# A hand-planned attention order with its copy queue, a start of its own for ten units, and MLP products placed between the last transposes

## The chip, the cores and the metric

The kernel runs on one core of a Trainium2 chip. The metric is the device time of one execution in microseconds (us). TensorE does the matmuls and transposes, VectorE and ScalarE read its results out of PSUM, GpSimd works on SBUF alone, and SyncE issues most of the transfers. Each engine works through its own list of instructions in the order in which the program was written; between engines there are only semaphores.

## The reference

```python
q_assign = argmax(q_n @ c_n)            # 16 clusters, per head
k_assign = argmax(k_n @ c_n)
mask = q_assign[:, :, :, None] == k_assign[:, :, None, :]
scores = where(mask, 0.125 * q @ k.T, -1e9)
attn_out = softmax(scores) @ v          # 2 batches, 8 heads, 768 x 64, fp32
x = attn_out as (1536, 512)
h = max(max(x @ w1, x @ w2), x @ w3);   x = h @ w_out           # 512 -> 768 -> 512
h = x @ w_in;  out = max(0.01 * h, h) @ w_out2                  # 512 -> 2048 -> 512
```

All of it is fp32, and the weights are read as 64-bit words and taken apart into two fp32r halves on the chip.

## The kernel before

The work has two parts. The attention part has 16 head slices, taken as 8 pairs of heads (0 to 7). A pair is 6 units, so there are 48 units (n = 0 to 47); a unit is 256 queries of one head against 768 keys. The MLP part then runs the two MLPs over three blocks of 512 tokens, each product as three fp32r matmuls (`three`, L226), with the weight units taken apart beside it (`Weights`, L104).

One unit passes through these steps, which the order tables name with letters. `S0`, `S1` (`scores`, L589, matmuls L601): two score blocks of 128 queries, each of four matmuls, two on the operands q1, k1 and two on q2, k2, which also carry the cluster rows that mask. `M` (`maxima`, L605): the row maximum on VectorE. `X` (`exps`, L610): exp on ScalarE with the sums. `R` (`inverse`, L619): two small VectorE instructions. `Q` (`normal`, L625): scaling on GpSimd. `T0`, `T2`, `T4` (`transposes`, L629): four TensorE transposes each. `E0`, `E2`, `E4` (`out_of_psum`, L640): their copies, by ScalarE, VectorE, ScalarE. `V` (`values`, L651, matmuls L657): 24 matmuls, once for two units. `Y` (`store`, L662): the copy to `acc`. The score blocks have two PSUM buffers (pool `ps_s`), so block i+2 waits for the exp of block i.

A pair is prepared before its first unit. `LD` and `LV` (`load_pair`, L337) load q, k and v from SyncE's queue; q and k have two buffers, v has three. `G`, `C`, `H`, `Na`, `Nb`, `W`, `FA`, `FB`, `O`, `P` (L472 to L518) find each token's cluster and end in the tile `oo`; they use one buffer `e` and one `oh`. `QH`, `KH`, `QL`, `KL` round q and k and form the rests. `D0` and `D1` (`operands`, L526, copies L530) copy the rounded tiles and `oo` into the operand tiles: 10 transfers each (a row with x2 in an order is two), from SyncE's queue. `w` takes one step at the weight unit 0 (`take_apart`, L681; each step is one or two instructions of `piece`, L136), and `F` (`fetch_pieces`, L675) issues the loads `raw` and `low` for it.

The order is written out in tables. `BEGIN` is the list up to the steady state, with dummy matmuls (`I2`, `I4`: `idle`, L769). `ORDER` has one string for each of the six places r of a unit in its pair: for each n the loop at L894 goes through string n % 6; `S0/-3` there means step S0 of unit n+3, and `KH+2` means KH of the pair two ahead. `ONCE` puts further steps ahead of a named one, `END` stands last. Nothing is reordered later (the schedule is manual), so the place of an item in these strings is its place on its engine's list. What an item waits for is the data and the buffers.

The lines of `ORDER` that matter here are r = 0 and r = 1, which hold `D0+1 ... LD+3 LV+2` and `D1+1`: SyncE's queue has the loads of q, k and v between the two halves of a pair's copies.

Of the kernel before, what the change touches and what calls it, by code (L numbers as in the profile page):

```python
# [17 lines left out]
P = 128  # L18
B, H, S, D = 2, 8, 768, 64
C = 16  # L20
NP = H // 2
NPAIR = B * NP
NQ = S // P
G = 256
# [10 lines left out]
SCALE = 0.125  # L35
BIG = 2.0**100
ORDER = (
    "R/-1 E2/1 X1/-2 Nb+2 D0+1 Q1/0 Q0/-1 R/-2 T4/1 S0/-3 T0/0 E4/1 S1/-3 E0/0 M0/-3 LD+3 LV+2 X0/-3 "
    "M1/-3 T2/0 T4/0 X1/-3 Q1/-1",
    "T0/0 S0/-3 Q0/-1 Y/4 E2/1 QH+2 T2/0 S1/-3 W+2 FA+2 M0/-3 D1+1 F+0 Q1/-1 M1/-3 R/-2 X0/-3 Q0/-2 V/2 "  # L40
    "E2/0 E4/1 X1/-3",
    "S0/-3 E0/1 w+0 Q1/-1 w+0 T4/1 KH+2 M0/-3 S1/-3 E4/1 M1/-3 R/-2 T0/0 QL+2 X0/-3 Y/3",
    "X1/-2 T2/1 T4/1 S0/-3 V/2 E0/1 Q0/-1 E4/1 S1/-3 FB+2 M0/-3 X0/-3 T0/0 E0/0 Q1/-1 E2/1 T2/0 M1/-3 "
    "S0/-4 T4/0 E2/0 T0/-1 R/-2",
    "X1/-2 S1/-3 T2/0 E4/1 G+3 E0/0 Q0/-1 Q1/-1 T4/0 M0/-3 X0/-3 R/-2 M1/-3 S0/-4 E2/0 X1/-3 C+3",
    "T0/0 S1/-3 E4/1 KL+2 O+2 H+3 Y/4 w+0 M0/-3 Q0/-1 M1/-3 Na+3 T2/0 E0/0 P+2 X0/-3 w+0 w+0 V/2",
)

BEGIN = (
    "Zaq LDq Zal Zak LDk Zaj Zam Gq I2 Gk Zar I2 Naq Nbq Wq FAq FBq Zbq UQ Zbk CQ LV0 I6 Nak "  # L50
# [3 lines left out]
)  # L54

END = "h h h V:47 h h Y:47 h"

ONCE = {
    "M1:3": "KL@1", "X1:3": "D0@1 F", "S1:5": "D1@1", "E0:4": "V:2 Y:2",
    "T0:46": "in x0 x1", "T0:47": "x2 x3 ph h", "T4:47": "h", "E4:47": "oh h",  # L60
}
WAYS = ("ADA", "ADA")
ENGINE = {"QH": "A", "QH@1": "P", "KH": "P", "KL": "P", "KL@0": "D", "W": "P", "W@1": "D"}
# [10 lines left out]
def clustered_attention_mlps(  # L74
# [124 lines left out]
    mlp, m = ctx.enter_context(ExitStack()), {}  # L199

    def open_inputs():

        m["w1"] = mlp.enter_context(tc.tile_pool(name="w1", bufs=1))
        xp = mlp.enter_context(tc.tile_pool(name="xp", bufs=1))
        m["xh"] = [xp.tile([P, KD, TB], F32R, name=f"xh{t}") for t in range(NTB)]
        m["xl"] = [xp.tile([P, KD, TB], F32R, name=f"xl{t}") for t in range(NTB)]

    def open_products():
        m["ps_h"] = mlp.enter_context(tc.tile_pool(name="ps_h", bufs=4, space=PSUM))

    def open_hidden():

        m["tp"] = mlp.enter_context(tc.tile_pool(name="tp", bufs=2))
        m["hp0"] = mlp.enter_context(tc.tile_pool(name="hp0", bufs=1))

    chunks = [[0], [1]] + [[u, u + 1] for u in range(2, U1 + U2, 2)]

# [86 lines left out]
    with ExitStack() as att:  # L304
# [32 lines left out]
        def load_pair(p, what="qkv", queue=nc.sync):  # L337
            s = st.setdefault(p, {})
            for x in what:
                if x == "v":  # L340
                    s["rv"] = vp.tile([P, NQ, 2, D], F32, tag="rv", name=f"rv{p}")
                    src = v[p].rearrange("p (t h d) -> p t h d", t=NQ, h=2)
                else:
                    s["r" + x] = raws.tile([P, S], F32, tag="r" + x, name=f"r{x}{p}")
                    src = (qT if x == "q" else kT)[p]
                queue.dma_start(out=s["r" + x], in_=src)
# [45 lines left out]
        def sims(p, j, spare):  # L392
            s = st[p]
            r = s[("rq", "rk")[j]]
            for t in range(NQ):
                nc.tensor.matmul(
                    spare[:, t * 2 * C : (t + 1) * 2 * C], r[:, t * P : (t + 1) * P],
                    cb[:, p % NP, :], start=True, stop=True,
                )
            if j == 0:  # L400
                s["m"] = sm.tile([P, NQ, 2, 2, 1], F32, tag="m1", name=f"m1_{p}")
                s["e"] = sm.tile([P, NQ, 2, 2, C], F32, tag="e", name=f"e{p}", bufs=1)
# [267 lines left out]
        def scrap(key):  # L670
            if key not in scraps:
                scraps[key] = ps_t.tile([P, 512], F32, tag="t", name=f"scrap{len(scraps)}")
            return scraps[key]
# [7 lines left out]
        def take_apart():  # L681

            if len(taken) < len(fetched):
                c = fetched[len(taken)]
                if c not in pieces:
                    pieces[c] = weights.piece(weights.raw.pop((0, c)), 0, wa, c)
                if next(pieces[c], None) is None:
                    taken.append(c)
# [67 lines left out]
        if True:  # L756
# [12 lines left out]
            def idle(n):  # L769
                for _ in range(n):  # L770
                    nc.tensor.matmul(warm, nought[:, 0:P], nought, start=True, stop=True)
# [42 lines left out]
            def start(op):  # L814

                if op[0] == "I":
                    idle(int(op[1:]))
                elif op[0] == "Z":
                    first_operands("ab".index(op[1]), op[2])
                elif op == "D2":  # L820
                    operands(0, 2, (1,))
                elif op in ("LDq", "LDk"):
                    load_pair(1, op[2], nc.scalar)
                elif op == "LV0":
                    load_pair(0, "v", nc.scalar)
                elif op in ("Gq", "Gk"):
                    sims(0, "qk".index(op[1]), scrap(op))
                elif op in ("Naq", "Nak"):
                    near_max(0, "qk".index(op[2]), scrap("G" + op[2]))
                elif op in ("Nbq", "Nbk"):  # L830
                    near_eq(0, "qk".index(op[2]))
                elif op in ("Wq", "Wk"):
                    weigh(0, nc.vector, "qk".index(op[1]))
                elif op in ("FAq", "FAk"):
                    first_max(0, "qk".index(op[2]))
                elif op in ("FBq", "FBk"):
                    first_eq(0, "qk".index(op[2]))
                elif op in ("UQ", "UK"):
                    onehot_up(0, "QK".index(op[1]), scrap(op))
                elif op == "CQ":  # L840
                    ps = scrap("UQ").bitcast(BF16)[D : D + C, 0:S]
                    nc.scalar.copy(st[0][0][1][D : D + C], ps)
                elif op == "CK":
                    ps = scrap("UK").bitcast(BF16)[D : D + C, 0:S]
                    up = slice(D, D + C)
                    nc.scalar.activation(
                        st[0][0][3][up], ps, AF.Identity, scale=gain[up], bias=base[up]
                    )
                elif op == "OT":
                    for h in range(2):  # L850
                        onehot_T(0, h, scrap(op)[:, 256 * h : 256 * h + 256])
                elif op in ("PA", "PB"):
                    h = "AB".index(op[1])
                    penalties(0, h, scrap("OT")[:, 256 * h : 256 * h + 256])
                elif op == "in":
                    until_scores.close()
                    open_inputs()
                elif op == "oh":
                    until_transposes.close()
                    open_hidden()  # L860
                elif op == "F":
                    fetch_pieces()
                elif op == "ph":
                    until_exps.close()
                    open_products()
                    st["first"] = hidden(0, 0)
                elif op == "h":
                    next(st["first"])
                elif op[0] == "x":
                    split_x(0, (int(op[1]),))  # L870
                else:
                    raise ValueError(op)

            NU = NPAIR * 2 * NG
            begun = BEGIN.split() + END.split()
            begun += ["V:1", "Y:1"]
# [17 lines left out]
            for n in range(-2 * NG, NU + 2 * NG):  # L894
                c, r = divmod(n, 2 * NG)
                for item in ORDER[r].split():
                    if "/" in item:
                        op, by = item.split("/")
                        if 0 <= n - int(by) < NU:
                            ordered(op, n - int(by))  # L900
                    else:
                        op, by = item.split("+")
                        if op in "wF" or 1 <= c + int(by) < NPAIR:
                            ordered(op, c + int(by))
            assert len(taken) == UW // WP

            for op in END.split():
                other(op)
# [70 lines left out]
```

## Time and profile before

| what | us |
|---|---|
| median of 3 executions (lowest, highest) | 731.91 (727.87, 734.37) |
| the profiled execution, its time | 730.9 |
| its span, from the first to the last instruction | 729.0 |
| TensorE busy in the span | 700.5 (96%) |
| mean granted TensorE clock, as a share of full speed | 0.980 |

The span is what the trace shows; 1.9 us of the profiled execution lie around it. A matmul's duration in the trace overlaps with that of the next one, so the chain of waits, which counts only what each one adds, is the better measure of what a group costs. A share of busy time under one, or a granted clock of 0.50 (1.2 GHz in place of 2.4 GHz), shows where TensorE loses time.

### The profile page before, as it was taken

To read this page: it belongs to the slowest core of one execution; us is meant where nothing else is said; L and a number is where in the kernel's file an instruction comes from. 1 tells how busy PE (TensorE), PEld (TensorE's weight loads), DVE (VectorE), ACT (ScalarE), POOL (GpSimd) and SP (SyncE) were. 2 spreads that over 40 slices of the span, in tenths; PEclk is the share of its full clock that TensorE was granted. 3 is DMA by queue.
4 is the path that set the end of the run, shared out by engine and by line. 5 is a ranking of instruction groups with operands and counts; after the bars stand their busy time and mean duration, and the time that the engine had idled before them with its cause. 6 is when DMAs were issued, how large, how long until landed. Compare 5 with 4: busy or idle time off the path is not lost.

```text
span 729.0 us, 10287 instructions
## 1 busy us (share of the span) xinstructions
PE 700.5 (96%) x3730; PEld 559.3 (77%) x3730; DVE 494.2 (68%) x898; ACT 337.5 (46%) x637; POOL 215.8 (30%) x195
## 2 busy tenths in 40 slices
PE   8678998899999989999999999999999999999997
PEld 5466776676777768888888888888888888888886
DVE  6576896777766529878887289878619954983222
ACT  6356776767867645523322124536434432432220
POOL 0445464555553311101110111223222322222220
PEclk9769999999999999999999999999999999999999
DMA  3873468355261005645555045416514541610112
GB/s 110 273 169 102 140 158 202 101 137 136 66 152 66 1 6 197 209 167 169 159 164 173 30 144 170 147 47 215 166 36 144 174 144 35 197 58 1 43 40 90
DMA packets 30081, 89.95 MB, mean 123 GB/s; under 512 B 4784, under 2 KB 5680, under 8 KB 30032
## 3 DMA queue, kind: packets, MB, share of 16 engines
q1 hardware_dynamic: 29600, 88.14, 40.6%
q10 hardware_dynamic: 432, 1.18, 0.5%
q8 instruction: 29, 0.48, 0.3%
q14 instruction: 20, 0.16, 0.1%
HBM read 68.16 MB, written 3.15 MB: 98 GB/s over the span
## 4 chain that ended last, share of the span: by engine, by line
PE 90%; DVE 3%; ACT 2%; DMA 2%; SPq 1%; POOL 1%; issue 1%; ACTq 0%; POOLq 0%; DVEq 0%
PE h L231 13%; PE h L233 13%; PE h L232 13%; PE o L657 10%; PE y L233 8%; PE s L601 8%; PE y L231 8%; PE y L232 8%; PE t L634 7%; DMA k<-oo 2%; SPq L530 1%; ACT ee L613 1%; DVE mx L607 1%; POOL ee L627 1%; PE g L476 1%
## 5 line engine op out<-in xcount | busy, mean ns | idle before, releaser
L265 POOL TENSOR_TENSOR hl<-a,hh 128x512 fp32r<-128x512 f32 x66 | 92.0, 1394 | 353.3 <-ACT hh L264 345.2
L231 PE MATMUL h<-xh,wh 128*128 128x512 f32 x408 | 159.1, 390 | 0.0
L233 PE MATMUL h<-xh,wl 128*128 128x512 f32 x408 | 158.8, 389 | 0.0
L232 PE MATMUL h<-xl,wh 128*128 128x512 f32 x408 | 158.7, 389 | 0.0
L627 POOL TENSOR_SCALAR ee<-ee,rs 128x768 f32<-128x768 f32 x96 | 96.0, 1012 | 135.6 <-DVE rs L622 47.3
L607 DVE TENSOR_REDUCE mx<-s 128x1 f32<-128x768 f32 x96 | 91.3, 954 | 52.4 <-PE s L601 50.9
L601 PE MATMUL s<-k,q 128*128 128x512 f32 (+3 forms) x392 | 99.4, 376 | 14.0 <-DMA k<-oo 8.8
L231 PE MATMUL y<-hh,wh 128*128 128x512 f32 x264 | 102.7, 389 | 0.0
L232 PE MATMUL y<-hl,wh 128*128 128x512 f32 x264 | 102.7, 389 | 0.0
L233 PE MATMUL y<-hh,wl 128*128 128x512 f32 x264 | 102.7, 389 | 0.0
L264 ACT CAST hh<-a 128x512 fp32r<-128x512 f32 x66 | 41.1, 623 | 127.5 <-DVE a L258 76.7
L613 ACT ACTIVATE ee<-s,mx 128x768 f32<-128x768 f32 x96 | 86.6, 903 | 24.3 <-DVE mx L607 23.4
L634 PE MATMUL t<-idf,ee 128*128 128x128 f32 x576 | 81.8, 279 | 8.1 <-POOL ee L627 7.0
L231 PEld LDWEIGHTS h<-xh,wh 128*128 128x128 f32 x408 | 76.6, 188 | 16.5 <-issue 0.8
L233 PEld LDWEIGHTS h<-xh,wl 128*128 128x128 f32 x408 | 76.6, 188 | 16.0
L232 PEld LDWEIGHTS h<-xl,wh 128*128 128x128 f32 x408 | 76.6, 188 | 15.7
L601 PEld LDWEIGHTS s<-k,q 128*128 128x128 f32 (+1 forms) x392 | 63.3, 201 | 29.2 <-ACT ee L613 10.7
L256 ACT COPY a<-h 128x512 f32<-128x512 f32 x66 | 38.6, 586 | 95.7 <-PE h L233 94.1
L634 PEld LDWEIGHTS t<-idf,ee 128*128 128x128 f32 x576 | 67.5, 143 | 19.4 <-POOL ee L627 8.7
L291 DVE TENSOR_TENSOR acc<-y,acc 128x512 f32<-128x512 f32 x72 | 48.6, 685 | 40.5 <-PE y L233 40.5
L260 DVE SCALAR_TENSOR_TENSOR a<-a,h 128x512 f32<-128x512 f32 x48 | 32.9, 684 | 61.8 <-ACT a L256 61.6
L647 ACT COPY et<-t 128x512 f32<-128x512 f32 x96 | 55.0, 592 | 42.1 <-PE t L634 42.0
(100 smaller groups left out, 847.3 us busy)
## 6 DMA issues: line engine op xcount, KB each, us to landing
raw<-in_w SPq DMA_DIRECT2D x56, 512.0 KB, 3.9
low<-in_w SPq DMA_DIRECT2D x56, 511.5 KB, 3.5
q<-qh SPq DMA_DIRECT2D x28, 192.0 KB, 4.2
k<-kh SPq DMA_DIRECT2D x28, 192.0 KB, 4.3
out_T<-acc SPq DMA_DIRECT2D x12, 256.0 KB, 2.0
rq<-in_qT SPq DMA_DIRECT2D x7, 384.0 KB, 5.0
rk<-in_kT SPq DMA_DIRECT2D x7, 384.0 KB, 3.6
rv<-in_v SPq DMA_DIRECT2D x7, 384.0 KB, 4.0
```

Source lines behind the costliest of these rows:

```text
L231: nc.tensor.matmul(ps, ah, bh, start=(k == 0), stop=False)
L232: nc.tensor.matmul(ps, ah, bl, start=False, stop=False)
L233: nc.tensor.matmul(ps, al, bh, start=False, stop=(k == n - 1))
L265: nc.gpsimd.tensor_tensor(hlo[:, f, :], a, hh[:, f, :].bitcast(F32), op=ALU.subtract)
L291: nc.vector.tensor_tensor(a, ps, a, op=ALU.add)
L601: nc.tensor.matmul(ps[:, lo:hi], a[:, c0 : c0 + P], b[:, lo:hi], start=start, stop=not start)
L607: nc.vector.tensor_reduce(mx, un[n]["s", i], axis=AX.X, op=ALU.max, negate=True)
L613: nc.scalar.activation(e, u.pop(("s", i)), AF.Exp, bias=u.pop(("m", i)), scale=1.0, accum_out=u["sum"][:, i, 0:1],)
L627: nc.gpsimd.tensor_scalar(e, e, un[n]["rs"][:, i : i + 1], 1.0, op0=ALU.mult, op1=ALU.mult)
L634: nc.tensor.transpose(ps[:, kk, i * P : (i + 1) * P], u["e"][i][:, (k + kk) * P : (k + kk + 1) * P], idf,)
L647: nc.scalar.copy(out, ps)
L657: nc.tensor.matmul(un[n]["o"][j * D : (j + 1) * D], v[:, t, j, :], done[p, g, j][:, t, :], start=(t == 0), stop=(t == NQ - 1),)
```

## The change

The tables are new. Of `ORDER`, two lines of the diff show the kind of change:

```diff
-    "R/-1 E2/1 X1/-2 Nb+2 D0+1 Q1/0 Q0/-1 R/-2 T4/1 S0/-3 T0/0 E4/1 S1/-3 E0/0 M0/-3 LD+3 LV+2 X0/-3 "
+    "S0/-3 w+0 X1/-2 T0/0 M0/-3 Q0/-1 S1/-3 M1/-3 Q1/-1 T2/0 E4/1 Y/3 D0+1 E0/0 E2/0 X0/-3 G+2 S0/-4",
```

`LD+3` now stands in r = 2, and in place of `LV+2` there is `LV+1` in r = 5; `D0+1` ends r = 0 and `D1+1` begins r = 1. `BEGIN` is written out up to the scores of unit 13, with its own place for each item of the units 0 to 9. The rest of the diff, cut to its core:

```diff
+AFTER = 10
-END = "h h h V:47 h h Y:47 h"
+END = "h h V:47 h h Y:47"
 ONCE = {
-    "M1:3": "KL@1", "X1:3": "D0@1 F", "S1:5": "D1@1", "E0:4": "V:2 Y:2",
-    "T0:46": "in x0 x1", "T0:47": "x2 x3 ph h", "T4:47": "h", "E4:47": "oh h",
+    "T0:45": "in x0 x1 x2 x3", "T0:46": "ph h h", "T4:46": "h h", "T0:47": "h", "T4:47": "h h",
+    "E4:47": "oh",
 }
...
     def open_inputs():
-        m["w1"] = mlp.enter_context(tc.tile_pool(name="w1", bufs=1))
...
+        m["tp"] = mlp.enter_context(tc.tile_pool(name="tp", bufs=2))
+        m["hp0"] = mlp.enter_context(tc.tile_pool(name="hp0", bufs=1))
...
     def open_hidden():
-        m["tp"] = mlp.enter_context(tc.tile_pool(name="tp", bufs=2))
-        m["hp0"] = mlp.enter_context(tc.tile_pool(name="hp0", bufs=1))
+        m["w1"] = mlp.enter_context(tc.tile_pool(name="w1", bufs=1))
...
                         if op in "wF" or 1 <= c + int(by) < NPAIR:
-                            ordered(op, c + int(by))
+                        if op in "wF":
+                            if n >= AFTER:
+                                do(op, 0)
```

In `ONCE`, `in` opens the MLP's input tiles, `x0` to `x3` split the first token block into its fp32r halves, `ph` opens the MLP's PSUM tiles, and each `h` is one step of three matmuls of the first product. The weights' home `w1` opens later and the hidden tiles' home earlier than before. No matmul of attention or of the MLPs is added or taken away; the dummy matmuls fall from 29 to 23.

What stands on three engines before and now:

VectorE (DVE) at the start, from the last rest of pair 0's operands on. `mx` is a row maximum (M), numbered by unit and block; `near1`, `e1`, `oh1` belong to the cluster search of pair 1, `ql1` to its rounding. Before:

```order
L364 TENSOR_TENSOR k2_0_1_227<-rk0_118,k1_0_1_226 64x768
L607 TENSOR_REDUCE mx0_0_273<-s0_263 128x1
L607 TENSOR_REDUCE mx0_1_279<-s1_266 128x1
L607 TENSOR_REDUCE mx1_0_301<-s2_296 128x1
L621 TENSOR_REDUCE rs0_307<-sums0_107 128x2
L622 RECIPROCAL rs0_307<-rs0_307 128x2
L607 TENSOR_REDUCE mx1_1_322<-s3_315 128x1
L497 TENSOR_REDUCE m1_1_312<-near1_324 128x24
```

Now:

```order
L374 TENSOR_TENSOR k2_0_1_227<-rk0_118,k1_0_1_226 64x768
L507 TENSOR_REDUCE m1_1_280<-near1_287 128x24
L513 TENSOR_TENSOR e1_281<-near1_287,m1_1_280 128x384
L371 SCALAR_TENSOR_TENSOR ql1_305<-rq1_189,qh1_283 128x768
L437 TENSOR_TENSOR e1_281<-e1_281,desc_104 128x384
L443 TENSOR_REDUCE m2_1_None_325<-e1_281 128x24
L457 TENSOR_TENSOR oh1_327<-e1_281,m2_1_None_325 128x384
L617 TENSOR_REDUCE mx0_0_354<-s0_263 128x1
L617 TENSOR_REDUCE mx0_1_367<-s1_266 128x1
```

Six instructions of pair 1's cluster search and rounding moved ahead of the first row maximum.

SyncE (SP) in the steady state, around the second half of pair 3's copies (`kl3`, `oo3`) and the load of v (`rv`). Before:

```order
L530 DMA q1_3_1_1153<-ql3_948 64x768
L346 DMA rq5_1192<-in_qT 128x768
L346 DMA rk5_1194<-in_kT 128x768
L346 DMA rv4_1196<-in_v 128x768
L530 DMA k2_3_0_1147<-kl3_1091 64x768
L530 DMA q2_3_0_1145<-oo3_1115 16x384 x2
```

Now:

```order
L356 DMA rv2_1044<-in_v 128x768
L137 DMA raw0_2_1101<-in_w 128x2048
L137 DMA low0_2_1103<-in_w 128x2046
L540 DMA q1_3_0_1146<-qh3_932 64x768
L540 DMA q2_3_0_1147<-qh3_932 64x768
L540 DMA k1_3_0_1148<-kh3_846 64x768 x2
L540 DMA q1_3_0_1146<-ql3_988 64x768
L540 DMA q1_3_1_1155<-qh3_932 64x768
L540 DMA q2_3_1_1156<-qh3_932 64x768
L540 DMA k1_3_1_1157<-kh3_846 64x768 x2
L540 DMA q1_3_1_1155<-ql3_988 64x768
L540 DMA k2_3_0_1149<-kl3_1051 64x768
```

The two halves of a pair's copies now follow one another, and the load of v stands ahead of both and is that of an earlier pair (2 in place of 4).

VectorE at the end of attention. `et` are copies of transposes (E2), `xl0` the split of the first token block, `rs46` and `rs47` the inverses of the last two units. Before:

```order
L649 COPY et44_3068<-t44_2_3045 128x512
L649 COPY et45_3077<-t45_2_3081 128x512
L222 TENSOR_TENSOR xl0_3104<-acc0_64,xh0_3101 128x512 x2
L621 TENSOR_REDUCE rs47_3116<-sums3_110 128x2
L622 RECIPROCAL rs47_3116<-rs47_3116 128x2
L649 COPY et46_3125<-t46_2_3119 128x512
L222 TENSOR_TENSOR xl0_3104<-acc0_64,xh0_3101 128x512 x2
```

Now:

```order
L659 COPY et44_3035<-t44_2_3030 128x512
L232 TENSOR_TENSOR xl0_3057<-acc0_64,xh0_3054 128x512 x4
L631 TENSOR_REDUCE rs46_3079<-sums2_109 128x2
L632 RECIPROCAL rs46_3079<-rs46_3079 128x2
L631 TENSOR_REDUCE rs47_3086<-sums3_110 128x2
L632 RECIPROCAL rs47_3086<-rs47_3086 128x2
L659 COPY et45_3084<-t45_2_3102 128x512
```

The four splits and the last inverse no longer stand behind the copy of unit 45's transposes.

## Rows read from the trace of the kernel before

**Rows 1.** Stages: stretch, length, busy us (PE, PEld, DVE, ACT, POOL), granted clock, DMA share, GB/s
```profile
16.00:62.00 46.00, 35.23 (x175) 25.17 (x175) 29.23 (x52) 21.31 (x44) 21.73 (x20) 0.78 0.76 209
62.00:91.00 29.00, 26.62 (x202) 20.74 (x206) 21.97 (x40) 21.93 (x45) 12.40 (x13) 1.00 0.33 97
91.00:121.00 30.00, 27.98 (x205) 21.26 (x198) 22.49 (x41) 20.23 (x44) 15.28 (x16) 0.94 0.68 170
121.00:152.00 31.00, 28.42 (x208) 21.46 (x207) 22.56 (x41) 21.27 (x45) 16.11 (x16) 0.94 0.65 150
152.00:181.00 29.00, 27.68 (x218) 20.96 (x215) 23.77 (x41) 21.54 (x45) 16.83 (x17) 1.00 0.46 116
206.60:256.00 49.40, 49.29 (x380) 39.00 (x379) 30.81 (x58) 36.32 (x77) 23.21 (x25) 1.00 0.25 64
256.00:272.00 16.00, 13.80 (x96) 9.41 (x95) 5.15 (x9) 6.16 (x14) 2.74 (x2) 1.00 0.00 1
272.00:729.00 457.00, 453.05 (x1998) 374.79 (x1998) 308.69 (x540) 160.56 (x280) 92.03 (x66) 1.00 0.38 125
```

**Rows 2.** TensorE's waits, whole span: us in total, times, longest
```profile
PE s L601 <- DMA k<-oo: 8.8, 5, 2.6
```

**Rows 3.** SyncE's own waits, 58 to 206 us, same columns
```profile
SPq L346 <- PE o L657: 63.6, 5, 17.1
```

**Rows 4.** Chain that ended last, around 112 us: start, us it adds, what
```profile
109.40 2.33 DMA k<-oo
...
112.39 4.43 PE o L657 x24
```

**Rows 5.** The same chain where nothing waits, at the full clock
```profile
242.30 0.71 PE s L601 x4
243.01 1.31 PE t L634 x12
...
246.17 2.74 PE o L657 x24
```

**Rows 6.** The same chain at the start, two pieces at the lower clock, the first V
```profile
33.42 1.65 PE s L601 x4
...
44.03 0.85 PE t L634 x4
...
59.22 2.79 PE o L657 x24
```

**Rows 7.** TensorE in order of time at the start, with its idle time before
```profile
16.38 1.85 PE L601 MATMUL s<-k,q 128*128 128x512 f32 x8 [0.54 <-ACT ee L613]
...
20.76 2.61 PE L634 MATMUL t<-idf,ee 128*128 128x128 f32 x11 [0.55 <-POOL ee L627]
...
29.87 0.33 PE L634 MATMUL t<-idf,ee 128*128 128x128 f32 x1 [3.46 <-POOL ee L627]
```

**Rows 8.** Single microseconds of the start, columns as in rows 1
```profile
23.00:24.00 1.00, 1.00 (x5) 0.90 (x4) 0.00 (x0) 0.59 (x1) 0.00 (x0) 0.53 0.95 359
...
47.00:48.00 1.00, 1.00 (x6) 0.90 (x6) 0.97 (x5) 0.81 (x2) 0.41 (x1) 0.58 0.45 108
```

**Rows 9.** VectorE in order of time at the start
```profile
19.50 0.55 DVE L497 TENSOR_REDUCE m<-near 128x24 f32<-128x384 f32 x1
...
20.75 1.17 DVE L427 TENSOR_TENSOR e<-e,desc 128x384 f32<-128x384 f32 x1
...
28.09 0.96 DVE L361 SCALAR_TENSOR_TENSOR ql<-rq,qh 128x768 fp32r<-128x768 f32 x1
```

**Rows 10.** ScalarE, in order of time: its last reading of pair 0's k
```profile
14.47 0.84 ACT L353 ACTIVATE k<-rk 64x768 fp32r<-64x768 f32 x1
```

**Rows 11.** Loads of k (`rk`) from issue to landing, first 100 us
```profile
DMA to landing us min/median/max: 3.3/3.7/6.2
```

**Rows 12.** The chain that ended last, at the end of attention
```profile
255.03 0.60 PE t L634 x4
...
261.39 0.98 PE t L634 x7
```

More of the change, by code (lines that the diff above doesn't have):

```diff
@@ L37 @@
 ORDER = (
-    "R/-1 E2/1 X1/-2 Nb+2 D0+1 Q1/0 Q0/-1 R/-2 T4/1 S0/-3 T0/0 E4/1 S1/-3 E0/0 M0/-3 LD+3 LV+2 X0/-3 "
[L39 to L46, printed above, removed]
[9 rows of a table added]
 )
 BEGIN = (
-    "Zaq LDq Zal Zak LDk Zaj Zam Gq I2 Gk Zar I2 Naq Nbq Wq FAq FBq Zbq UQ Zbk CQ LV0 I6 Nak "
[3 rows of a table removed]
-)
-END = "h h h V:47 h h Y:47 h"
+    "Zaq LDq Zal Zak LDk Zaj Zam Gq I2 Gk Zar I2 Naq Nbq Wq FAq FBq Zbq UQ Zbk CQ LV0 I6 Nak Nbk Wk FAk FBk  "
[12 rows of a table added]
+)
+AFTER = 10
+END = "h h V:47 h h Y:47"
 ONCE = {
-    "M1:3": "KL@1", "X1:3": "D0@1 F", "S1:5": "D1@1", "E0:4": "V:2 Y:2",
-    "T0:46": "in x0 x1", "T0:47": "x2 x3 ph h", "T4:47": "h", "E4:47": "oh h",
+    "T0:45": "in x0 x1 x2 x3", "T0:46": "ph h h", "T4:46": "h h", "T0:47": "h", "T4:47": "h h",
+    "E4:47": "oh",
 }
@@ L823, in start @@
                     load_pair(1, op[2], nc.scalar)
+                elif op == "w":
+                    take_apart()
                 elif op == "LV0":
@@ L902, in clustered_attention_mlps @@
                         op, by = item.split("+")
-                        if op in "wF" or 1 <= c + int(by) < NPAIR:
+                        if op in "wF":
+                            if n >= AFTER:
+                                do(op, 0)
+                        elif 1 <= c + int(by) < NPAIR:
                             ordered(op, c + int(by))
```

23 rows, old and new, of tables (BEGIN, ORDER) are left out of this document.

## The prediction

> **What bounds the kernel now.** I read the stages first, because 96% busy over the span hides where the rest is lost [rows 1]. From 272 us on TensorE is busy 453.05 of 457.00 us at full clock, with the same 1998 matmuls' worth of MLP work before and after the change, so nothing can be won there. The two pairs of attention from 206.6 to 256, for which nothing is prepared any more, are as dense: 49.29 of 49.40 us. What is lost lies in three places. From 16 to 62 us TensorE is busy 35.23 of 46.00 us, and at a mean clock of 0.78. From 62 to 181 us it is idle for 2.38, 2.02, 2.58 and 1.32 us in four stretches, 8.30 in all, and two of them have a clock of 0.94. From 256 to 272 us, where attention ends, it is idle for 2.2 us.
>
> Then the waits tell what stands behind the middle loss. TensorE waits five times for the copies of `oo` into the operands, 8.8 us in all [rows 2]. SyncE, which issues them, stood for 63.6 us in five waits on TensorE's V [rows 3]: that is `LV+2`, which wants a buffer of v that the pair before last still reads, and behind it in the queue stand the copies of `D1+1`. In the chain the wait ends in 2.33 us of transfer, and the V behind it takes 4.43 us [rows 4], where one at full clock takes 2.74 [rows 5]: the idle time let the clock fall to the lower level, which cost another 1.69 us. That happens in two of the stretches, the ones with 0.94.
>
> At the start it is a chain through all engines (score, maximum, exp, next score), with the clock on top. After 3.46 us without work [rows 7] the clock fell, and it was back only just before 48 us [rows 8]. At the lower level a score block adds 1.65 us to the chain and a group of four transposes 0.85 [rows 6], against 0.71 and 1.31/3 = 0.44 [rows 5].
>
> **The middle.** The change takes `LV+2` away from between the copies. `LV+1` in r = 5 asks for a buffer whose last V lies a whole pair back, so it should not wait, and `LD+3` now stands behind `D1+1`. SyncE is not tied to the other engines' places: once D0 is free of `rv` it can issue both halves as soon as their data is there, well ahead of the first score of the pair. The waits for `oo` then go with the lower clock they cause: at most 8.30 us of idle time and 2 x 1.69 = 3.4 us of clock, 11.7 us. What is late next is ScalarE, with 20 to 22 busy us of each 29 to 31, and the loads `raw` and `low`, which still stand ahead of D0 in two pairs and wait for the weight steps `w`. I leave 3.2 us for such waits, 0.8 per stretch, as the new order can't be as dense as the pairs without preparation. That gives 8.5 us; the bounds are 11.7 and 4, the last if the copies are late in every other pair.
>
> **The start.** Here the change first costs something. VectorE has six instructions of pair 1 ahead of the first maximum, which stood there alone. They wait for the search of pair 1: ScalarE is through with pair 0's operands at 14.47 + 0.84 = 15.3 us [rows 10]; the copy C (about 0.5, from the 0.55 of another pass over 384 columns [rows 9]) and three transposes (1.31/4 = 0.33) end at 16.2. The six take 4 x 0.55 + 0.96 + 1.17 = 4.3 us [rows 9], so the first maximum begins at 20.5 and ends at 21.5, a pass over 768 columns taken at 0.96. With an exp of 0.9 (ScalarE's 0.84 for 768 columns [rows 10]) unit 1's first score comes at 22.4 us, where it came at 16.38 [rows 7]: 6.0 us later. TensorE has G of pair 2 to do ahead of that score. Its load can begin when ScalarE lets go of pair 0's k at 15.3, and lands 3.7 us later, at worst 6.2 [rows 11]; at 19.0 it is hidden behind VectorE's six instructions, at 21.5 it would cost up to 2 us. The first `raw` and `low` now load at once, beside the loads of pair 1 (2.1 MB, some 10 us at the 209 GB/s of this stage [rows 1]); they are through before the search of pair 1 needs its data, so I count nothing for them.
>
> In return the units that follow are free of pair 1's and 2's search. I look at the place where 18 score blocks and one V are done: before that is 59.22 + 2.79 = 62.0 us [rows 6]. Now it is just behind unit 8's first score. A unit without V needs 2 x 0.71 + 1.31 = 2.73 us of TensorE, a unit with its half of a V 4.10 [rows 5]; I take 3.5, a little over the middle, since exps and VectorE's weight step take turns with TensorE. Seven units give 24.5, the V 2.74, the last block about 0.8: 22.4 + 28.0 = 50.4 us, or 11.6 us early, if the clock stays up. It won't: TensorE has little to do from about 17 to 22 us, as before the fall at 30 us [rows 7], and the dummy matmuls that followed are gone. At the lower level a unit needs 2 x 1.65 + 3 x 0.85 = 5.85 us [rows 6], 2.35 more. The full clock came back once just before 24 us, soon after TensorE's work had set in again, and once just before 48, some 17 us after it [rows 7, 8]; I take two units, 4.7 us. The start then gains 11.6 - 4.7 = 6.9 us. Bounds: 11.6 with no fall at all, and nothing or a loss if it lasts.
>
> At the first of these returns the row shows that nearly all of TensorE's work ahead of 23.4 us was transposes, 11 in a row [rows 7], with one score block behind them, and that the clock rose before 24 us [rows 8]. The Trainium skill, "TensorE: Matmul & The Clock Gate", Part 4 on the PE-mode transpose, says that transposes do not count as busy in the same way, so that they don't bring the full clock. The row does not settle it, since the scores came last. By the rule the first units, in which transposes alternate with thin scores, would hold the lower level much longer than my two units, and the time would be that of the first rival below; by the row it is the forecast's.
>
> **The end.** In the chain, from 255.03 to 261.39 + 0.98 = 262.4 us [rows 12] pass 7.3 us, in which TensorE does eight groups of transposes (8 x 0.44 = 3.5) and three MLP matmuls (3 x 453.05/1998 = 0.7). So 3.1 us are waits, most of them for Q of unit 47, whose inverse stood on VectorE behind the copy of unit 45's transposes. Now both inverses stand ahead of that copy, and two, two, one and two steps of MLP products fill the places between the transposes; the four splits (VectorE) are done beside the V of unit 43. I leave 0.8 us for the first Q, which the splits now hold up, and count 2.3; bounds 3.1 and 0.5. The buffers that move cost nothing: the weight home `w1` is first written behind the last V, as before, and the MLPs' matmuls stay packed [rows 1].
>
> **Sum.** 6.9 + 8.5 + 2.3 = 17.7 us off the profiled execution's 730.9, which is 713.2; I say 713. The median of the three executions is 1.0 us above the profiled one, within their own scatter, so I add nothing.
>
> **The rivals.** *The lower clock lasts through five units.* For it speaks how long it took to come back before 48 us [rows 7, 8] and the skill's rule; against it that the units are dense at the lower level, when a unit needs 5.85 us of TensorE alone. The start then gives 11.6 - 5 x 2.35 = -0.2, and the time is 730.9 + 0.2 - 8.5 - 2.3 = 720.3, say 720.
>
> *The new steady order only trades waits.* The copies are on time, but ScalarE (up to 75% busy in these stretches [rows 1]) or the loads ahead of D0 hold TensorE up as long as `oo` did. For it speaks that each of six strings was changed throughout; against it the dense pairs at 206.6, where ScalarE was as busy (36.32 of 49.40) and TensorE waited for nothing. The middle then gives 0: 730.9 - 6.9 - 2.3 = 721.7, say 722.
>
> *Slower: the lower clock feeds on itself.* The place is the first two pairs. Seven units at 5.85 in place of 3.5 and a V at 4.43 turn 11.6 us of gain into 11.6 - 16.5 - 1.7 = -6.6. Each unit from there on needs 5.85 + 4.43/2 = 8.07 us against 4.10, so 4.0 more. Against the 10.8 us of the other two stages the kernel is slower by 1% once the lower level lasts through unit 10; through unit 12 it is 6.6 + 5 x 4.0 = 26.6 later, and the time 730.9 + 26.6 - 10.8 = 746.7, say 747. For it speaks the stretch from 31 to 47 us; against it that every spell of the lower level in the trace ended while TensorE had work.
>
> **How the numbers follow.** Forecast 0.58, own range 705 to 721 (the start between 2 and 11.6, the middle between 5 and 11.7); long lower clock 0.19; traded waits 0.14; slower 0.09. 1%, 7.3 us, is about what a measurement of this kernel can tell from no change; it lies at 724.6 against the median. The forecast lies below that throughout, the two rivals at 720 and 722 with part of their own spread above it (0.13 and 0.09 below, 0.06 and 0.05 within), the last 0.06 beyond 739.2 and 0.03 within: faster 0.80, same 0.14, slower 0.06. A range from 704 to 727 takes in the forecast, most of the two middle cases, and leaves the last one out.
>
> **What would show it.** Right: SyncE's waits on V between 58 and 206 us are gone, TensorE's waits for `oo` fall from 8.8 us to under 2, no V takes over 4 us behind unit 12, unit 1's first score begins at 21 to 24 us, the state of 62.0 us is reached between 51 and 60, and the span is 15 to 20 us shorter. Wrong: a granted clock near 0.5 over more than 15 us in the start, or stretches from 62 us on in which TensorE is idle for 2 us per pair on other waits, ScalarE's exps above all.

## The result and the profile after

The changed kernel takes 712.55 us (median of 4 executions, 708.46 to 714.18) against 731.4 us of the kernel before (4 executions, 727.87 to 734.37). The ratio is 0.9736, with a 95% interval of 0.9674 to 0.9798: 18.9 us, 2.6%, faster. The forecast was 713.0. The profiled execution of the changed kernel, which the rows below show, is the slowest of its four.

| what | before, us | after, us |
|---|---|---|
| the profiled execution, its time | 730.9 | 714.18 |
| its span | 729.0 | 712.3 |
| TensorE busy in the span | 700.5 | 694.0 |
| mean granted clock | 0.980 | 0.985 |

The windows of the kernel after, columns as in [rows 1], then two windows of its start:

```profile
16.00:62.00 46.00, 40.46 (x258) 30.75 (x257) 36.61 (x64) 32.58 (x66) 21.84 (x23) 0.89 0.46 115
62.00:91.00 29.00, 25.77 (x175) 19.68 (x173) 17.25 (x32) 16.59 (x35) 12.78 (x12) 0.88 0.54 151
91.00:121.00 30.00, 30.00 (x234) 23.27 (x232) 25.29 (x46) 24.34 (x51) 16.61 (x17) 1.00 0.79 193
121.00:152.00 31.00, 31.00 (x243) 24.41 (x243) 26.56 (x48) 24.59 (x50) 19.41 (x20) 1.00 0.71 199
152.00:181.00 29.00, 29.00 (x226) 22.38 (x222) 23.68 (x43) 22.72 (x49) 14.87 (x15) 1.00 0.52 119
...
206.60:256.00 49.40, 46.27 (x333) 35.42 (x334) 23.53 (x44) 27.57 (x57) 14.22 (x16) 0.97 0.00 1
...
22.00:28.00 6.00, 4.42 (x14) 3.31 (x15) 2.82 (x6) 3.44 (x8) 0.81 (x1) 0.50 0.99 220
28.00:33.00 5.00, 5.00 (x23) 4.57 (x23) 3.15 (x6) 2.46 (x5) 2.66 (x4) 0.58 0.67 157
```

From 91 to 181 us TensorE has no idle time at all and the clock is full; in [rows 1] it was idle 2.02, 2.58 and 1.32 us there, at 0.94 in two of the stretches. The start has 258 matmul records where it had 175. But there is a new hole from 62 to 91 us, 3.23 us of idle time and a clock of 0.88 (0.12 of 29 us is another 3.5), and another one before 256 us, 3.13 us.

The waits of TensorE over the whole span name them (columns as in [rows 2]):

```profile
PE s L611 <- ACT ee L623: 3.4, 4, 1.5
PE s L611 <- DMA k<-oo: 3.2, 1, 3.2
PE o L667 <- ACT acc L673: 2.6, 1, 2.6
PE g L486 <- DMA rk<-in_kT: 1.5, 1, 1.5
```

Of the five waits for `oo` [rows 2] one is left. In the load of v, SyncE's waits on V [rows 3] are gone. Of its waits on TensorE one has grown, on a score; over the whole span the kernel before had 2.7 us of it in five waits, now it is:

```profile
SPq L540 <- PE s L611: 23.3, 7, 14.9
```

TensorE in order of time, the instructions that the text speaks of (start, duration, what, idle time before it):

```profile
19.14 0.84 PE L486 MATMUL g<-rk,cb 128*32 128x384 f32 x4 [1.51 <-DMA rk<-in_kT]
...
22.07 1.65 PE L611 MATMUL s<-k,q 128*128 128x512 f32 x4 [0.76 <-ACT ee L623]
...
70.88 0.98 PE L611 MATMUL s<-k,q 80*128 80x512 f32 x2 [3.17 <-DMA k<-oo]
...
75.63 3.27 PE L667 MATMUL o<-et,rv 128*64 128x256 f32 x24
...
80.43 2.78 PE L611 MATMUL s<-k,q 128*128 128x512 f32 x12
...
86.89 2.81 PE L667 MATMUL o<-et,rv 128*64 128x256 f32 x24
...
193.31 2.81 PE L667 MATMUL o<-et,rv 128*64 128x256 f32 x24
...
237.68 4.15 PE L667 MATMUL o<-et,rv 128*64 128x256 f32 x24 [2.58 <-ACT acc L673]
```

86.89 and 193.31 are the fifth and the seventeenth V. Up to either of them both kernels have run the same number of score blocks, transposes and V's, so they can be set against the same instructions of the kernel before. The first row is the place of its second scores of unit 0, of which more below:

```profile
31.74 3.33 PE L601 MATMUL s<-k,q 128*128 128x512 f32 x8
...
94.92 2.81 PE L657 MATMUL o<-et,rv 128*64 128x256 f32 x24
...
212.28 2.81 PE L657 MATMUL o<-et,rv 128*64 128x256 f32 x24
```

With the ends of the spans that gives three sections: up to the fifth V the change is 94.92 - 86.89 = 8.0 us ahead, from there to the seventeenth it wins 117.36 - 106.42 = 10.9, and from there to the end it loses 518.99 - 516.72 = 2.3. The sum is 16.6, the difference of the spans 16.7. At the fifth V the kernel before had done one more pair's G and `near` (11 matmuls, some 1.3 us of busy time), so at equal work the first section wins 6.7 us and the second 12.2.

**A repeat that the forecast had not seen.** Both kernels compute the two score blocks of unit 0 twice, and nothing reads the second ones. `BEGIN` calls the first ones SA0:0 to SB1:0; the loop that goes through `ORDER` skips what is in the list `begun`, and looks there for S0:0 and S1:0. Before, the second blocks ran at 31.74 us, in the lower clock. Now the written start ends with unit 13's first score, the loop comes to S0:0 only then, and the second blocks run at about 81 us (the group of 12 matmuls at 80.43 holds them and one other block). They read the operands of pair 0's first head, so one of the four buffers of each operand tile (pool `opn`: two heads of two pairs) stays taken until then. SyncE's wait of 14.9 us is a wait for such a buffer, in the copies of pair 2's second head. It did not last until the second blocks ran. It ended at 60.92 us, 20 us ahead of them, beside the last score block that reads pair 1's first head, that of unit 10; first SyncE's transfers, then that block:

```profile
45.48 0.79 SPq L540 DMA_DIRECT2D q<-ql  x1
60.92 1.10 SPq L540 DMA_DIRECT2D q<-qh  x2
```

```profile
60.30 0.95 PE L611 MATMUL s<-k,q 128*128 128x512 f32 x4
```

So with one buffer held, three go round, and pair 2's second head had to take over the one that unit 10 left; the trace doesn't name buffers, so that last step is read from the order and the times. Behind the late copies stands TensorE's wait of 3.17 us, with the lower clock after it.

### The profile page after: what moved, and what is told of

Same layout as the page of the kernel before. It is cut to its first block, busy times and chain, and to the rows that moved or that the text cites. A ratio compares the mean times of both kernels' runs of the same rounds, so it can differ in the third digit from the quotient of the medians.

```text
span 712.3 us, 10323 instructions
## 1 busy us (share of the span) xinstructions
PE 694.0 (97%) x3723; PEld 557.6 (78%) x3724; DVE 491.2 (69%) x898; ACT 338.8 (48%) x637; POOL 209.8 (29%) x195
## 4 chain that ended last, share of the span: by engine, by line
PE 94%; DVE 2%; ACT 2%; DMA 1%; issue 1%; SPq 0%; POOL 0%; ACTq 0%; DVEq 0%; POOLq 0%
PE h L241 13%; PE h L243 13%; PE h L242 13%; PE s L611 10%; PE o L667 9%; PE t L644 9%; PE y L243 8%; PE y L242 8%; PE y L241 8%; PE g L486 1%; ACT ee L623 1%; DMA rk<-in_kT 1%; DVE mx L617 1%; DMA k<-oo 0%; PE near L502 0%
## 5 line engine op out<-in xcount | busy, mean ns | idle before, releaser
L637 POOL TENSOR_SCALAR ee<-ee,rs 128x768 f32<-128x768 f32 x96 | 90.7, 959 | 85.9 <-DVE rs L632 59.1
L611 PE MATMUL s<-k,q 128*128 128x512 f32 (+3 forms) x392 | 97.5, 373 | 6.7 <-ACT ee L623 3.4
L644 PE MATMUL t<-idf,ee 128*128 128x128 f32 x576 | 80.0, 279 | 0.2
L667 PE MATMUL o<-et,rv 128*64 128x256 f32 x576 | 69.3, 391 | 2.6 <-ACT acc L673 2.6
```

Of the source, the lines that this page charges most:

```text
L611: nc.tensor.matmul(ps[:, lo:hi], a[:, c0 : c0 + P], b[:, lo:hi], start=start, stop=not start)
L637: nc.gpsimd.tensor_scalar(e, e, un[n]["rs"][:, i : i + 1], 1.0, op0=ALU.mult, op1=ALU.mult)
L644: nc.tensor.transpose(ps[:, kk, i * P : (i + 1) * P], u["e"][i][:, (k + kk) * P : (k + kk + 1) * P], idf,)
L667: nc.tensor.matmul(un[n]["o"][j * D : (j + 1) * D], v[:, t, j, :], done[p, g, j][:, t, :], start=(t == 0), stop=(t == NQ - 1),)
```

## The experiments

All twelve kernels were measured in 5 rounds, each beside the kernel before (medians of 731.87, 732.19 and 730.12 us in the three groups of runs). Lines of the diffs are against the kernel after, unless the text says otherwise. The positions of the fifth and the seventeenth V and the end of the span are from the profiled execution of each. The changed kernel has four executions, from 708.46 to 714.18 us; those of experiments 4, 6, 7 and 8 overlap with them, so there a difference of medians is not clear of the scatter by itself. The place of the fifth V scatters too: in experiments 4 and 7, which are like the changed kernel up to there, it is 0.7 and 2.5 us earlier.

| kernel | median, us | 5th V | 5th to 17th V | 17th V to end | span |
|---|---|---|---|---|---|
| before | 731.4 | 94.92 | 117.36 | 516.72 | 729.0 |
| after | 712.55 | 86.89 | 106.42 | 518.99 | 712.3 |
| 1 no second scores | 706.05 | 78.32 | 106.44 | 519.34 | 704.1 |
| 2 second scores on pair 2 | 706.48 | 80.53 | 106.41 | 517.66 | 704.6 |
| 3 before, no second scores | 730.45 | 92.45 | 117.55 | 516.70 | 726.7 |
| 4 splits later | 708.98 | 86.22 | 106.44 | 515.54 | 708.2 |
| 5 loads between | 731.86 | 85.03 | 126.98 | 517.69 | 729.7 |
| 6 dummies | 709.42 | 82.38 | 106.42 | 519.00 | 707.8 |
| 7 old end | 710.19 | 84.42 | 106.44 | 517.04 | 707.9 |
| 8 old start | 712.35 | 87.48 | 106.52 | 519.70 | 713.7 |
| 9 old order | 722.51 | 87.44 | 119.13 | 514.43 | 721.0 |
| 10 old start, no second scores | 712.88 | 85.44 | 106.51 | 517.95 | 709.9 |
| 11 no second scores, splits later | 702.45 | 79.56 | 106.44 | 515.60 | 701.6 |
| 12 as 11, with dummies | 700.69 | 77.22 | 106.42 | 515.56 | 699.2 |

**1. Without the second scores.** Left out: unit 0's second score blocks, which are not read.

```diff
-            begun += ["V:1", "Y:1"]
+            begun += ["V:1", "Y:1", "S0:0", "S1:0"]
```

> The changed kernel without the second computation of unit 0's two score blocks. The tables ask for S0 and S1 of unit 0 once in BEGIN (as SA and SB) and once more in the loop behind it; nobody reads the second pair. Theory A (it holds buffers): in the changed kernel it stands behind unit 13's first block, so pair 0's operand buffers stay taken until then, the second half of pair 2's copies waits 14.9 us for a buffer, the scores of unit 12 wait 3.2 us for oo and the clock falls. A expects 3.2 us of wait, some 2.5 us of lower clock and 2 x 0.7 us of blocks to go: 7 us, about 705.5. Rival (only work): the copies are late for another reason and only the two blocks go, 1.4 us: about 711.

706.05 us (705.47 to 706.5), ratio 0.9654 (0.9631 to 0.9677): 6.5 us under the changed kernel. In the windows the hole is gone, and of SyncE's waits on a score 4.2 us are left; first the window, then the row of SyncE's waits over the whole span, then the copies that began at 60.92 us before:

```profile
62.00:91.00 29.00, 29.00 (x229) 22.25 (x229) 24.27 (x42) 22.73 (x48) 14.86 (x14) 1.00 0.59 155
```

```profile
SPq L540 <- PE s L611: 4.2, 4, 1.7
```

```profile
46.55 1.19 SPq L540 DMA_DIRECT2D q<-qh  x2
```

The 6.5 us agree with the 3.2 us of idle time and 3.5 us of clock that the window from 62 to 91 us had lost.

**2. The same two blocks at the same place, on pair 2's operands.** They too are not read; this leaves the work and takes away the hold.

```diff
+                if f"{op}:{at}" in ("S0:0", "S1:0"):
+                    again(int(op[1]))
...
```

> The changed kernel with the two unread score blocks of unit 0 computed in the same place on pair 2's operands instead, so that the work stays and pair 0's buffers are free after unit 5. Theory A (it holds buffers) expects the wait for oo of 3.2 us and its lower clock to go and the 1.4 us of blocks to stay: about 707. Rival (only work) expects no change: 712.5.

706.48 us (706.0 to 707.63), ratio 0.9663 (0.964 to 0.9687). So the 6 us are the price of the held buffer. The work of the blocks (2 x 0.71 in the chain [rows 5]) shows as 0.4 in the medians, whose ranges overlap. In the profiled executions the fifth V comes 2.2 us later than in experiment 1 and the last section is 1.7 shorter, for a reason that the last part of this text shows.

**3. The kernel before, without them** (the edit of 1, in the kernel before).

> The kernel before without the second computation of unit 0's two score blocks. There they stand at 31.74 us, at the lower clock, 1.65 us each, and hold no buffer that anyone waits for. If TensorE sets the pace at that place, 3.3 us go and the time is about 728; if the chain through VectorE and ScalarE does, or the load of pair 2, under 1 us: 731. Either way it says how much of the changed kernel's lead at the start comes from having moved these two blocks out of the stretch of low clock.

730.45 us, ratio 0.9984 (0.9963 to 1.0006): no difference that can be told from none. There the repeat stood early, and no run shows that it held anything that was wanted.

**4. The four splits behind the V of unit 43.** At the end of attention the changed kernel has `x0` to `x3` ahead of that V.

```diff
-    "T0:45": "in x0 x1 x2 x3", "T0:46": "ph h h", "T4:46": "h h", "T0:47": "h", "T4:47": "h h",
+    "T0:45": "in", "V:43": "x0 x1 x2 x3", "T0:46": "ph h h", "T4:46": "h h", "T0:47": "h", "T4:47": "h h",
```

> The changed kernel with the four splits of the first token block (x0 to x3) moved from ahead of T0 of unit 45 to ahead of V of unit 43, that is on ScalarE behind the store Y of unit 41 and on VectorE behind the last two inverses. Theory: V of unit 43 waited 2.58 us for that store, which stood behind the four casts, and then ran at the lower clock, 4.15 us in place of 2.74: 4.0 us go, about 708.5. Rival: the casts then hold up the copies E0 and E4 of unit 45 or the first MLP products by as much, and the time stays at 712.

708.98 us (707.24 to 710.12), ratio 0.9694 (0.9671 to 0.9716), 3.6 us less. What it mends is seen on ScalarE in the kernel after, in order of time, ahead of the V at 237.68:

```profile
235.19 2.16 ACT L231 CAST xh<-acc 128x512 fp32r<-128x512 f32 x4
237.26 0.37 ACT L673 COPY acc<-o 128x256 f32<-128x256 f32 x1
```

The store of an earlier V stands behind the four casts, and the V of unit 43 waits for the buffer which that store frees. With the splits later the same V, on TensorE, reads:

```profile
234.97 2.81 PE L667 MATMUL o<-et,rv 128*64 128x256 f32 x24 [0.51 <-ACT acc L673]
```

2.07 us less of a wait, and 2.81 in place of 4.15: 3.4 us, and the last section of the table is 3.45 shorter. Experiment 11 against experiment 1 gives the same 3.6 us, with ranges that lie apart.

**5. The two loads back between D0 and D1.** Nothing else of the new order is changed.

```diff
-    "S0/-3 w+0 X1/-2 T0/0 M0/-3 Q0/-1 S1/-3 M1/-3 Q1/-1 T2/0 E4/1 Y/3 D0+1 E0/0 E2/0 X0/-3 G+2 S0/-4",
+    "S0/-3 w+0 X1/-2 T0/0 M0/-3 Q0/-1 S1/-3 M1/-3 Q1/-1 T2/0 E4/1 Y/3 D0+1 LD+3 LV+2 E0/0 E2/0 X0/-3 G+2 S0/-4",
```

> The changed kernel with its loads of q, k and v put back to where they stood: LD+3 and LV+2 between D0+1 and D1+1, so that from pair 3 on the second half of a pair's copies waits on SyncE's queue for a buffer of v again. Theory of the forecast (that queue made the middle slow): the waits for oo and the V at the lower clock come back in three or four pairs, 2.2 to 4 us each, and the time rises by about 8.5 us to 721. Rival (the other moves of the order made the gain): the copies are issued late and nobody waits, 713 to 715.

731.86 us, ratio 1.0005 (0.9983 to 1.0026): the whole gain of the change is gone, more than either theory had said. Three views of it: TensorE's waits, SyncE's waits, and four windows.

```profile
PE s L611 <- DMA k<-oo: 14.3, 5, 3.7
```

```profile
SPq L356 <- PE o L667: 47.2, 4, 17.8
```

```profile
91.00:121.00 30.00, 27.26 (x201) 21.03 (x194) 22.80 (x40) 20.35 (x44) 16.04 (x15) 0.94 0.74 187
121.00:152.00 31.00, 27.28 (x201) 21.23 (x200) 22.63 (x40) 20.33 (x42) 14.20 (x15) 0.94 0.60 154
152.00:181.00 29.00, 26.24 (x180) 20.42 (x180) 20.78 (x35) 18.01 (x38) 13.41 (x14) 0.88 0.44 104
181.00:206.60 25.60, 22.73 (x164) 16.66 (x161) 17.88 (x32) 17.04 (x36) 12.62 (x13) 0.93 0.29 69
```

Four waits for `oo` are back, and SyncE stands at the load of v again, as in [rows 3]. The first of the five is still that of the held buffer:

```profile
70.04 0.67 PE L611 MATMUL s<-k,q 80*128 80x512 f32 x2 [2.23 <-DMA k<-oo]
```

From 91 to 206.6 us TensorE is idle for 12.1 us (115.6 less 103.5 busy), which is the four waits, and the clock costs up to another 9 (0.06 of 30, 0.06 of 31, 0.12 of 29 and 0.07 of 25.6 us): 21 us, where the table has 126.98 - 106.42 = 20.6. With the old order the four waits come to 7.7 us (experiment 9). The tables suggest why they are longer here: the last V of a pair, which frees the buffer of v, stands in r = 2 of the new order and in r = 1 of the old one, while the next pair's first score stands in r = 3 of both. No run tests that.

**6. Twenty-six dummy matmuls in the start's gaps.**

```diff
-    "PA G@2 W@1 FA@1 FB@1 KL@1 D2 D0@1 C@2 M0:0 H@2 X0:0 S0:1 M1:0 O@1 Na@2 X1:0 P@1 S1:1 D1@1 M0:1 M1:1 R:0  "
+    "PA I12 G@2 W@1 FA@1 FB@1 KL@1 D2 D0@1 C@2 M0:0 I4 H@2 I4 X0:0 S0:1 M1:0 O@1 Na@2 X1:0 P@1 S1:1 I6 D1@1 M0:1 M1:1 R:0  "
```

> The changed kernel with 26 dummy matmuls of 512 columns in TensorE's gaps of the start (12 ahead of G of pair 2, 4 on either side of H, 6 behind the second score of unit 1), so that the clock has no idle stretch to fall after. Theory of the forecast (the lower level costs two units, 4.7 us): the clock stays at full level from 16 to 33 us and the time falls by 3 to 5 us, to 708 to 710. Rival (the chain through VectorE and ScalarE sets the pace there): the clock stays up and the time stays at 712.

709.42 us (706.63 to 710.6), ratio 0.9688 (0.9658 to 0.9718), 3.1 us less, as the first theory has it; experiment 12 gives the better size. The window of the start shows that the clock no longer fell:

```profile
16.00:62.00 46.00, 44.03 (x300) 31.57 (x303) 38.71 (x69) 33.95 (x69) 21.96 (x23) 1.00 0.51 126
```

**7. The old end** (`END`, the last entries of `ONCE` and the places of the two homes as before).

```diff
-END = "h h V:47 h h Y:47"
+END = "h h h V:47 h h Y:47 h"
...
-    "T0:45": "in x0 x1 x2 x3", "T0:46": "ph h h", "T4:46": "h h", "T0:47": "h", "T4:47": "h h",
-    "E4:47": "oh",
+    "T0:46": "in x0 x1", "T0:47": "x2 x3 ph h", "T4:47": "h", "E4:47": "oh h",
```

> The changed kernel with the end of the kernel before: its ONCE entries from unit 46 on, its END and its homes for the MLP's tiles. The traces put the new end 1.1 us behind the old one at equal work (the last score block 17.7 us earlier than before, the last V with its products 16.6 us earlier): that reading expects 711.5. The forecast's reading (the new end is worth 2.3 us) expects 715.

710.19 us (707.38 to 711.79), ratio 0.9704 (0.9673 to 0.9735). That is below both expectations: with this order the old end is no worse than the new one, and by the profiled executions better. In the table's last section it is 1.95 us shorter (2.4 in the medians, whose ranges overlap). Some 1.3 us of that are the clock: the V of unit 43 runs at 2.81 us here and at 4.15 in the changed kernel. Where that V stays at the full clock with the new end (experiments 2, 5 and 10), the section is 517.66 to 517.95, 0.6 to 0.9 us longer than with the old one.

**8. The old start** (`BEGIN` and its entries of `ONCE` as before, and the weight steps from the first n on).

```diff
-AFTER = 10
+AFTER = -100
...
+    "M1:3": "KL@1", "X1:3": "D0@1 F", "S1:5": "D1@1", "E0:4": "V:2 Y:2",
```

> The changed kernel with the start of the kernel before: its BEGIN, its ONCE entries for units 1 to 5, and the weight steps of ORDER from the first unit on; ORDER and the end are the new ones. At equal real work the new start is 12.7 us ahead in the traces, but it carries the second scores of unit 0 behind it, which cost 6.5 us when they were taken out. That reading expects 712.5 + 12.7 - 6.5 = 718.7. The forecast's size of the start (6.9 us) expects 713.

712.35 us (711.45 to 715.69), ratio 0.9738 (0.9705 to 0.9771): the new start, as it stands, is worth nothing that can be told from the scatter, where the traces had suggested 6 us. With the start of before TensorE has no wait for `oo` at all; the repeat stands early there.

**9. The old order**, with the new start, end and homes.

```diff
-    "S0/-3 w+0 X1/-2 T0/0 M0/-3 Q0/-1 S1/-3 M1/-3 Q1/-1 T2/0 E4/1 Y/3 D0+1 E0/0 E2/0 X0/-3 G+2 S0/-4",
...
+    "R/-1 E2/1 X1/-2 Nb+2 D0+1 Q1/0 Q0/-1 R/-2 T4/1 S0/-3 T0/0 E4/1 S1/-3 E0/0 M0/-3 LD+3 LV+2 X0/-3 "
...
```

> The new start, end and homes with the steady order of before. A (the forecast's size of the middle): the order is worth about 8.5 us, so 712.5 + 8.5 = 721. B (the order is worth what moving its two loads back cost, 19.3 us): 730 to 732, with four or five waits for oo of 2 to 4 us and a V at 3 us or more behind each. C (the order nets nothing, as the start with its held operands spoils what it wins): 712 to 714.

722.51 us (718.42 to 724.24), ratio 0.9884 (0.9845 to 0.9923). That is 10.0 us above the changed kernel, near A. TensorE's waits:

```profile
PE s L611 <- DMA k<-oo: 10.2, 5, 2.6
```

One of the five, 2.46 us, is again that of the held buffer. Its middle section is 119.13 us, 1.8 longer than that of before, where two V's took 4.50 us; here a third one fell to the lower clock (4.38 us at 194.48). Its last section is 514.43, 2.3 shorter than with the old end.

**10. The old start, without the second scores** (8 with the edit of 1; it and the two that follow leave out the same blocks, which nobody reads).

> The start of before, with the new order and end, and without unit 0's second score blocks, which nobody reads. A (the new start is worth 5 to 6 us, and the second scores' hold of pair 0's operands ate that): the old start loses only the work of the two blocks, as in the kernel before (1.4 us), so 712.35 - 1.4 = 711, and 5 us above the changed kernel without them (706.05). B (the new start is worth nothing of itself): 706.

712.88 us (711.98 to 715.65), ratio 0.977 (0.9731 to 0.9809): A. Against experiment 1 the new start is worth 6.8 us; the ranges lie far apart.

**11. Without the second scores and with the splits later** (1 and 4 together).

> The changed kernel without the second score blocks and with the four splits of the MLPs' first step moved behind the V of unit 43. A (two separate places, the gains add up): 712.55 - 6.50 - 3.57 = 702.5. B (what the start wins is partly given back at the end, or the other way round): 704 to 706.

702.45 us (701.82 to 703.47), ratio 0.962 (0.9583 to 0.9657): A, the two gains add up.

**12. The same with the dummies** (1, 4 and 6 together).

> As the last one, and with 26 dummy matmuls in the gaps of the start. A (the lower clock from 22 to 33 us is a cost of its own, which the dummies take away whether pair 0's operands are held or not): 712.55 - 6.50 - 3.57 - 3.13 = 699.4. B (the dummies' 3 us came only from the units that the held operands delay): 702 to 703.

700.69 us (700.34 to 701.4), ratio 0.9595 (0.9558 to 0.9631), the fastest of all. The dummies bring 1.8 us here, with ranges that lie apart: between A and B. The 3.1 of experiment 6 hang on the four executions of the changed kernel. Its window from 62 to 91 us:

```profile
62.00:91.00 29.00, 29.00 (x228) 22.21 (x225) 24.36 (x42) 23.05 (x48) 15.18 (x14) 1.00 0.59 157
```

## Why the prediction was right or wrong

The time came out as forecast, 713.0 against 712.55, and that was partly luck. By the sections of the profiled executions, with the 1.3 us of G and `near` put where the work is done, start, middle and end were 6.7, 12.2 and -2.3, where the forecast had 6.9, 8.5 and 2.3: the middle gave 3.7 more, the end 4.6 less, and the start came out by two errors that cancel.

**The middle: right mechanism, too small.** The load of v ahead of the second half of the copies is what held TensorE up; putting the loads back (experiment 5) brings the waits and the lower clock back, and without them the pairs are dense. The mis-sized step is "I leave 3.2 us for such waits, 0.8 per stretch": from 91 to 181 us there are none, and the gain was a little over the upper bound of 11.7. The loads `raw` and `low` and ScalarE, named as late next, held TensorE up nowhere in these windows, which refutes the rival of traded waits for the steady state.

**The start: the right number for the wrong reasons.** The first score of unit 1 came at 22.07 us, forecast 22.4, in the way described: six instructions ahead of the first maximum. G of pair 2 waited 1.51 us for its load, inside the "up to 2 us" of the text. The lower clock lasted through five score blocks, from 22 us to just behind 32 (a mean of 0.58 over the five us from 28): two and a half units, where "I take two units" stood. So the rival of five units fell. The price of 4.7 us that the forecast put on this was too high: the dummies, which keep the clock up, win 1.8 us in the clearest pair of medians and 3.1 in the other. By the fifth V they are 2.0 to 4.5 us ahead of the three kernels that are alike up to there (82.38 against 84.42, 86.22 and 86.89). The units after it were quicker than the 3.5 us taken: the work that the kernel before had done at 62.0 us (16 score blocks that are read, 14 groups of transposes, one V, three G of q and of k) was done here at the end of this piece of the chain, 12.7 us earlier:

```profile
48.75 0.58 PE t L644 x4
```

Then the lead was lost. The step that failed is "I look at the place where 18 score blocks and one V are done": two of the 18 were unit 0's blocks a second time, and the place named for the kernel after, behind unit 8's first score, has 17. The forecast did not see that the two are a repeat, that they move from 31.74 to about 81 us with the written start, and that until then they hold a buffer of each operand tile. Experiments 1 and 2 price that at 6.5 and 6.1 us. Without it the new start is worth 6.8 us (experiment 10 against 1), with it nothing that shows (8). So the 6.7 us of the first section are not the 6.9 of the forecast come true. The new order alone reaches the fifth V at 87.48, the new start alone at 87.44, both together at 86.89, and both without the second scores at 78.32: against the 94.92 of before each of the two is worth some 7.5 us there, and the hold eats one of them.

**The end: failed.** The clause "the four splits (VectorE) are done beside the V of unit 43" left out that each split also has a cast on ScalarE. The four casts took 2.16 us ahead of a store for which that V was waiting. With the old order, where that V had no such wait, the new end does bring what was forecast: 516.72 - 514.43 = 2.3 us (the profiled execution of experiment 9 against before). With the new order it costs 0.6 to 0.9 us, and some 2 where the V also falls to the lower clock (experiment 7). With the splits behind the V it gains again: 515.54 us.

**What the text named as signs.** SyncE's waits on V were gone, as said. The waits for `oo` fell from 8.8 us to 3.2, not under 2; the one that is left is the hold. No V was to take over 4 us behind unit 12: one did, at 237.68, by the splits. The state of 62.0 us was to come between 51 and 60: it came at 49.3. The span was to be 15 to 20 us shorter: 16.7. The rival on the slow side had the lower clock feed on itself through the first two pairs; it ended just behind 32 us, while TensorE was busy without a gap (the window from 28 us above).

**Transposes and the clock.** From 22.07 us to the rise just behind 32 TensorE ran score blocks and three small matmuls, and from 29.7 us on eight transposes as well; the lower level did not outlast the units in which transposes and thin scores alternate, and the time that the first rival would have given, 720, did not come. The Trainium skill, "TensorE: Matmul & The Clock Gate", Part 4 on the PE-mode transpose, says that transposes do not count as busy in the same way. The rise came behind both kinds of work, so this trace does not settle that rule.

**What stays open.** Whether the dummies bring more in one kernel (3.1 us) than in the other (1.8) can't be told from the scatter of the changed kernel. Parts undone one at a time cost -0.2 (start), 10.0 (order) and -2.4 us (end) and don't add up to 18.9, for the reason given at the fifth V and because the new end is good in one order and bad in the other; there is no single split of the gain.

## What to carry to other kernels

When an order is written by hand, follow not only who waits for data but who is the last reader of each buffer: two score blocks of 0.71 us each cost 6 us more where they held a buffer that the copies of the next pair but one would have had. In a list that is issued in order, a load that waits for a buffer should not stand ahead of copies that are due sooner; putting two loads back between the copies of each pair cost 19 us here (experiment 5), with SyncE standing at one of them, the load of v. And count matmuls against what is computed: 98 score blocks (392 matmuls, four to a block) where 96 are needed pointed to the repeat in the trace of before already.

## What the runs showed of the hardware that was not expected

The same wait can cost the clock or not. The V of unit 43 waited exactly 2.58 us in several kernels. In experiment 1 it then ran at the lower level, 4.50 us; in experiment 10, after the same wait and beside the same order, at the full one, 2.81:

```profile
229.14 4.50 PE L667 MATMUL o<-et,rv 128*64 128x256 f32 x24 [2.58 <-ACT acc L673]
```

```profile
236.33 2.81 PE L660 MATMUL o<-et,rv 128*64 128x256 f32 x24 [2.58 <-ACT acc L666]
```

So some 1.7 us of such a wait's price come and go between executions (here of two kernels that are alike at this place). The table shows it in all seven kernels in which that V waited 2.58 us: the last section is 517.66 to 517.95 us where the V stayed at 2.81 (experiments 2, 5 and 10) and 518.99 to 519.70 where it took 4.15 to 4.50 (after, 1, 6 and 8). Against that, the middle section takes 106.41 to 106.52 us in all ten kernels that have the new order with its loads in place, whatever their start: once TensorE waits for nothing, hardly anything scatters.
